# Forgetting attention with a SwiGLU block: more buffers for V's loads and a newly planned order of loads and units

## The chip, the cores and the metric

The kernel runs on one core of one Trainium2 chip. The metric is device time in microseconds (us) of one execution. Five engines work side by side, each through its own list of instructions in order: PE (TensorE, matmuls), DVE (VectorE), ACT (ScalarE), POOL (GpSimd) and SP (SyncE, which here only starts transfers). Semaphores join them.

## The reference, cut to what matters

There are 8 batches of 8 heads, a sequence of 576 and a head size of 64. The FFN has 4608 tokens (8 times 576), a model width of 512 (the 8 heads side by side) and an inner width of 1536.

```python
scores = (q @ k.T) / sqrt(D)
cum    = cumsum(log(clip(f, 1e-4, 1)), axis=-1)
scores = where(causal, -1e9, scores + cum[:, None] - cum[None, :])
attn   = exp(scores - max(scores)); attn = attn / (sum(attn) + 1e-9)
x      = (attn @ v), heads side by side: (4608, 512)
g      = x @ w_gate
out    = (g * sigmoid(g) * (x @ w_val)) @ w_out
```

## The kernel before, in words

**Units.** A pair `p` (0 to 31) is two heads of one batch; batch `b` has pairs 4b to 4b+3. Its 576 rows are cut into blocks of 64, both heads stacked on 128 partitions. A unit of attention is a pair and a half `g`: `g` = 0 are blocks 0 to 3, `g` = 1 are blocks 4 to 8. For a pair the kernel loads K, Q (`kf`, `qf`, line 409) and the cumulated gates spread over partitions (`cb`, line 418), casts K and Q to bf16 (`kb`, `qb`, lines 434 to 438), transposes them on PE (line 452) and copies them to `kt` and `qz` (lines 464, 466). Then, by unit:

- PE forms the scores in banks `sp` (line 498) and adds the mask (line 502).
- DVE adds the gates and takes the row minimum of the negated scores (`t`, line 526).
- ACT takes the exponential and the row sum (`e`, line 546).
- DVE or ACT adds the small constant to the sums (lines 560, 562), and DVE inverts (line 564).
- POOL, or ACT for early pairs, normalizes into `pk` (lines 580, 582).
- `pk` is transposed into `pT`: on PE for pairs 0 to 7 (line 612, copied by line 617), by a transposing transfer for later ones (line 595).
- PE multiplies with V (`vt`) into `tx` (line 638), and DVE or ACT copies the result into `xT` (line 662).

V comes in five pieces of up to 128 rows for each batch (`vf`, line 678), which POOL casts into `vt` (line 682).

Pair 0's `cb` is the exception: it is not transferred but spread by a matmul on the chip (line 393, copied by line 397). All other `cb` are read back from DRAM, where line 378 puts the cumulated gates.

**FFN.** The tokens are cut into tiles of 256, 256, seven times 512, 256, 128 and 128. For each tile PE computes gate and value products (`wg`, `wv`, line 720), ACT a tanh (line 726), DVE two products (lines 728, 731), PE the output product (line 748), and ACT or DVE copies it out (lines 755, 757), from where SP stores it (line 760). A tile can begin when all four pairs of its batch have written its rows. The weights arrive as bf16 through casting transfers that POOL starts (lines 695, 699): gate and value in four pieces each, cut at columns 0, 256, 512, 1024 and 1536 (named `wg0`, `wg2`, `wg4`, `wg8` by their first block of 128 columns; likewise `wv`), and the output weights in three.

**What sets the order.** All of this is first recorded as operations with a duration, a priority and candidate engines. `Plan.order` then plays the machine forward: it keeps a time for each engine and for the two transfer paths, gives each operation the earliest start that its inputs, its buffers and its engine allow, and so picks engine, buffer and place. The result is written out as a fixed order for each engine. So a constant that changes a planned time can move any operation after it. The constants that matter here:

- `COLD` (line 17): until this planned time, in ns, PE's durations count double.
- `STARTUP` (line 260): the order of the first loads. `p4` is K and Q of pair 4, `c4` its `cb`, `v03` piece 3 of V of batch 0, `wg4` a weight piece, `f9` the gates.
- `AHEAD` (line 250): a load of this list is planned no sooner than the one so many places ahead of it has landed. It is a rule of the plan, not a wait in the program.
- `NUDGE` (line 264): what is added to the priority of a unit. `a16.1` is attention of pair 16, half 1; `q12` loads and preparation of pair 12; `f8` gates of FFN tile 8; `o4` output of tile 4.
- `WAIT` (line 266): ns added to the planned start of a unit when the planner chooses between operations.

Buffers are real waits: a load into `vf` waits until the cast has read what the buffer held. `cm` (lines 299 and 475 to 483) holds gate sums with the mask added for pairs from `MFROM` on; `MFROM` is 32.

Of the kernel before, what the change touches and what calls it, by code (L numbers as in the profile page):

```python
# [8 lines left out]
F32 = mybir.dt.float32  # L9
# [4 lines left out]

BIG = 1.0e9
HUGE = 3.0e38
COLD = 25000
SLOW = 1.03


# [12 lines left out]
class Plan:  # L33
# [29 lines left out]
    def order(self):  # L63
# [72 lines left out]
        while ready:  # L136
# [18 lines left out]
            s -= o.bias.get(e, 0)  # L155
            if e == "PE" and s < COLD:
                dur *= 2
# [42 lines left out]
def kernel(  # L200
# [12 lines left out]
    B, H, S, D = q.shape  # L213
# [3 lines left out]
    P = 128  # L217
    QB = 64
    NB = S // QB
# [27 lines left out]
    NDIRECT = 0  # L247
    NSEL = 1
    MOST = (("p", 1), ("o", 2), ("f", 3))
    AHEAD = 7  # L250
    BEHIND = 6
    BOTH = 8
    LATER = {"DVE": 100}
# [3 lines left out]
    SOON = 8  # L257
    BACK = 4
    CBACK = 5
    STARTUP = "p0 f9 p1 c1 p3 p2 c2 v00 c3 wv0 wg2 wg0 wv2 v04 wv4 v01 v03 c4 wg4 v02 p4 wg8 wv8 v10 f0 p5 p6 c5 v14 c6 wo0 p7 wo4 v12 v13 v11 c7 wo8"  # L260
    HEAD = "10 00 20 30 11 01 31 21"


    NUDGE = "a10.0:1 a13.0:2 a15.0:-1 a15.1:-0.5 a16.1:-2 a20.0:-1 a21.0:1 a23.1:-1 a26.1:0.5 a27.1:-1.5 a28.0:1 a29.0:1 a31.1:10 f3:-4 f4:-7 f5:1 f6:2 f7:4.5 f8:4 f9:8 o6:-2.5 o8:2 q11:-2 q15:4 q22:5.5 q24:2.5"

    WAIT = ""
    ORDER = [(int(u[0]), int(u[1])) for u in HEAD.split()]
    ORDER += [(p, g) for p in range(len(ORDER) // 2, NPAIR) for g in (1, 0)]
    at = {u: n for n, u in enumerate(ORDER)}
# [8 lines left out]
    def bufs(name, shape, dtype, n, space=None):  # L278
        pl.pool(name, [(space or sb).tile(shape, dtype, name=f"{name}{x}") for x in range(n)])
# [16 lines left out]
    bufs("qz", [P, NB, 2, QB], BF16, 4)  # L296
    bufs("cb", [P, S], F32, 5)
    bufs("t", [P, S], F32, 4)
    bufs("cm", [P, NB, QB], F32, 2)
    for i in range(0, NB, 2):  # L300
        bufs(f"e{i}", [P, QB * (i + 2)], F32, 2)
    bufs("eo", [P, 512], F32, 4)
# [4 lines left out]
    for n in ("pk", "pT"):  # L307
        both[n] = [sb.tile([P, sum(NSL), P], BF16, name=f"{n}{x}") for x in range(2)]
        pl.pool(n + "1", [x[:, 0:NSL[1], :] for x in both[n]])
        pl.pool(n + "0", [x[:, NSL[1]:, :] for x in both[n]])  # L310
    bufs("vf", [P, H, D], F32, 2)
    bufs("vt", [P, 5, H, D], BF16, 2)
    bufs("th", [P, 512], F32, 3)
    bufs("hh", [P, 512], BF16, 18)
# [463 lines left out]
    line = []  # L778
    for x in STARTUP.split():
        n = int("".join(c for c in x if c.isdigit()))  # L780
# [14 lines left out]
    for n, o in enumerate(line):  # L795
        o.prio = -100 + n * .1
        if n >= AHEAD:
            o.after.append(line[n - AHEAD])
        if "POOL" in o.engs:
# [29 lines left out]

    nudge, leave = ({k: float(v) for k, v in (y.split(":") for y in x.split())} for x in (NUDGE, WAIT))  # L830
    for o in pl.ops:
# [38 lines left out]
```

## Time and profile before

| | us |
|---|---|
| median of 3 runs (lowest, highest) | 421.09 (419.6, 421.73) |
| the profiled execution's own time | 420.02 |
| its span, first to last instruction | 418.2 |

| engine | busy us | share of the span |
|---|---|---|
| PE (matmul) | 398.1 | 95% |
| DVE | 325.3 | 78% |
| ACT | 311.0 | 74% |
| POOL | 252.6 | 60% |

The profile is one execution. Busy time of PE includes the tail of each matmul, under which the next has begun, so it hides gaps shorter than that tail. "Idle before" a group of instructions is followed by what ended the wait. SP's own waits are those of its queue: while SP waits for one transfer's buffer or for an earlier transfer, all transfers behind it in its list wait too.

### The profile page before, as it was taken

How to read it: one execution, taken by the hardware profiler on the slowest of the kernel's cores; microseconds unless marked ns; L12 is line 12 of the kernel's file. 1: busy time of each engine (PE TensorE's matmuls, PEld its weight loads, DVE VectorE, ACT ScalarE, POOL GpSimd, SP SyncE). 2: the span in 40 equal slices, each digit the busy share in tenths (PEclk: the TensorE clock that was granted, in tenths of full speed). 3: DMA queues.
4: the chain of work that ended last, by engine and by line, in shares of the span. 5: the costliest groups of instructions: out<-in, count | busy, mean ns of one | idle time of the engine just before them, and what ended most of it. 6: DMA issues, size and time to landing. Idle time of an engine off the chain costs nothing.

```text
span 418.2 us, 9999 instructions
## 1 busy us (share of the span) xinstructions
PE 398.1 (95%) x3304; PEld 231.8 (55%) x3304; DVE 325.3 (78%) x1044; ACT 311.0 (74%) x875; POOL 252.6 (60%) x460
## 2 busy tenths in 40 slices
PE   1679999999999999999999999999999999999996
PEld 1446887665555555555555555555454444447875
DVE  4589999989998979889998979898866474553532
ACT  4689999999999978888987979899886332223321
POOL 7399977999788983886795787759784000000000
PEclk9999999999999999999999999999999999999999
DMA  7999999997999999999999999979976401001111
GB/s 176 203 166 235 220 214 206 224 236 183 204 229 212 232 197 237 204 237 199 225 216 226 228 235 210 234 189 208 221 155 146 88 2 51 25 27 50 52 52 52
DMA packets 143029, 72.22 MB, mean 173 GB/s; under 512 B 117761, under 2 KB 129793, under 8 KB 142977
## 3 DMA queue, kind: packets, MB, share of 16 engines
q1 hardware_dynamic: 136804, 66.27, 73.8%
q0 software_dynamic: 5808, 4.72, 7.7%
q10 hardware_dynamic: 364, 0.59, 0.6%
q8 instruction: 26, 0.43, 0.4%
q14 instruction: 27, 0.21, 0.2%
HBM read 47.04 MB, written 9.58 MB: 135 GB/s over the span
## 4 chain that ended last, share of the span: by engine, by line
PE 77%; DMA 7%; ACT 6%; POOL 4%; DVE 3%; issue 2%; SPq 0%; POOLq 0%; DVEq 0%; ACTq 0%
PE gv L720 38%; PE gv L748 20%; PE sp L498 8%; PE tx L638 5%; DMA kf<-in_k_dram 3%; PE tx L452 3%; POOL pk L582 3%; PE gv L612 2%; DMA pT<-pk 2%; DVE t L526 2%; ACT eo L546 2%; ACT e L546 2%; PE sp L502 1%; DMA cb<-cum_f 1%; DMA cum_f<-t 1%
## 5 line engine op out<-in xcount | busy, mean ns | idle before, releaser
L526 DVE CUSTOM_DVE_ANT_0 t<-sp,cb 128x512 f32<-128x512 f32 (+7 forms) x288 | 130.9, 475 | 13.5 <-PE sp L502 5.0
L582 POOL TENSOR_SCALAR pk<-e,lr 128x128 bf16<-128x128 f32 (+3 forms) x190 | 100.1, 530 | 32.7 <-DVE lr L564 15.1
L720 PE MATMUL gv<-xT,wv 128*128 128x512 bf16 (+2 forms) x576 | 111.4, 326 | 0.0
L720 PE MATMUL gv<-xT,wg 128*128 128x512 bf16 (+2 forms) x576 | 111.3, 326 | 0.0
L728 DVE SCALAR_TENSOR_TENSOR th<-th,gv 128x512 f32<-128x512 f32 x108 | 73.9, 685 | 43.7 <-ACT th L726 43.2
L748 PE MATMUL gv<-wo,hh 128*128 128x512 bf16 (+1 forms) x444 | 107.5, 374 | 0.0
L726 ACT ACTIVATE th<-gv 128x512 f32<-128x512 f32 x108 | 64.0, 592 | 42.1 <-PE gv L720 40.3
L546 ACT ACTIVATE e<-t,tm 128x448 f32<-128x448 f32 (+4 forms) x160 | 88.5, 555 | 4.6 <-DVE tm L526 3.9
L731 DVE TENSOR_TENSOR hh<-th,gv 128x512 bf16<-128x512 f32 x108 | 73.4, 685 | 9.0 <-PE gv L720 5.5
L498 PE MATMUL sp<-kt,qz 128*128 128x448 bf16 (+6 forms) x320 | 72.8, 295 | 3.8 <-DVE tm L526 3.7
L582 POOL TENSOR_SCALAR pk<-eo,lr 128x256 bf16<-128x256 f32 (+3 forms) x128 | 67.7, 530 | 12.4 <-DVE lr L564 4.9
L546 ACT ACTIVATE eo<-t,tm 128x256 f32<-128x256 f32 (+3 forms) x128 | 71.2, 557 | 4.3 <-DVE tm L526 2.2
L720 PEld LDWEIGHTS <-wv 128*128 128x128 bf16 x576 | 49.3, 98 | 34.8
L720 PEld LDWEIGHTS <-wg 128*128 128x128 bf16 x576 | 49.2, 98 | 35.0
L748 PEld LDWEIGHTS <-hh 128*128 128x128 bf16 x444 | 39.7, 98 | 37.1
L502 PE MATMUL sp<-mask,ident 128*128 128x64 bf16 x288 | 48.2, 197 | 0.0
L755 ACT ACTIVATE ot<-gv 128x512 f32<-128x512 f32 (+1 forms) x33 | 19.1, 581 | 36.7 <-PE gv L748 34.7
L498 PEld LDWEIGHTS <-qz 128*128 128x128 bf16 x320 | 31.0, 101 | 19.8 <-DVE qz L466 1.3
L436 POOL TENSOR_SCALAR qb<-qf 72x1024 bf16<-72x1024 f32 x30 | 31.2, 1041 | 8.8 <-DMA qf<-in_q_dram 6.1
L502 PEld LDWEIGHTS <-ident 128*128 128x128 bf16 x288 | 27.2, 100 | 15.2 <-issue 3.9
L546 ACT ACTIVATION_READ_ACCUMULATOR e<-t,tm 128x1 f32 x160 | 30.7, 192 | 0.0
L638 PE MATMUL tx<-pT,vt 128*64 128x320 bf16 (+4 forms) x448 | 29.4, 266 | 0.7 <-DMA pT<-pk 0.3
(60 smaller groups left out, 379.7 us busy)
## 6 DMA issues: line engine op xcount, KB each, us to landing
out_dram<-ot SPq DMA_DIRECT2D x35, 256.0 KB
kf<-in_k_dram SPq DMA_DIRECT2D x31, 288.0 KB
qf<-in_q_dram SPq DMA_DIRECT2D x31, 288.0 KB
cb<-cum_f SPq DMA_DIRECT2D x62, 144.0 KB
vf<-in_v_dram SPq DMA_DIRECT2D x32, 256.0 KB
wo<-in_moe_w_out_dram POOLq DMA_DIRECT2D x3, 512.0 KB, 9.2
vf<-in_v_dram SPq DMA_DIRECT2D x8, 128.0 KB
wv<-in_moe_w_val_dram POOLq DMA_DIRECT2D x2, 512.0 KB, 8.3
```

The source lines that it names most:

```text
L436: eng[e].tensor_scalar(dst, src, -scale, 1.0, op0=ALU.mult, op1=ALU.mult)
L498: nc.tensor.matmul(sp[:, o:o + z - a], qz[:, i, :, :].rearrange("p h r -> p (h r)"), kt[:, a:z], start=True, stop=not last or p >= MFROM)
L502: nc.tensor.matmul(sp[:, o - QB:o], ident, mask, start=False, stop=True)
L526: nc.vector.tensor_tensor_reduce(out=pl.buf(tk)[:, a:z], in0=pl.buf(sk)[:, o:o + z - a], in1=pl.buf(("cm", p))[:, i, :] if own else pl.buf ...
L546: nc.scalar.activation(pl.buf(ek)[:, :L], pl.buf(tk)[:, :L], AF.Exp, bias=pl.buf(("tm", p, g))[:, 0, i:i + 1], scale=-1.0, accum_out=pl.bu ...
L582: eng[e].tensor_scalar(dst, src, r, 1.0, op0=ALU.mult, op1=ALU.mult)
L638: nc.tensor.matmul(xo[r, 0:QB * n], vt[:, c, 2 * hp + h, :], pT[:, a:a + n, 64 * h:64 * h + 64], start=(c == 0), stop=(c == nch - 1))
L720: nc.tensor.matmul(pl.buf(bk)[:, j * n:j * n + n], wt[:, ko, fc * P:fc * P + P], xT[:, ko, x0:x0 + n], start=ko == 0, stop=ko == KD - 1)
L726: pl.op({"ACT": 487}, lambda e, u=u: nc.scalar.activation(pl.buf(("th", t, u)), pl.buf(("wg", t, u)), AF.Tanh, scale=0.5), [("wg", t, u)], ...
L728: pl.op({"DVE": 605}, lambda e, u=u: nc.vector.scalar_tensor_tensor(pl.buf(("th", t, u)), pl.buf(("th", t, u)), 1.0, pl.buf(("wg", t, u)), ...
L731: pl.op({"DVE": 605}, lambda e, u=u: nc.vector.tensor_mul(pl.buf(("hh", t, u)), pl.buf(("th", t, u)), pl.buf(("wv", t, u))), [("u", t, u), ...
L748: nc.tensor.matmul(pl.buf(bk)[:, 0:z - a], hh[:, (fc % nf) * n + ms * P:(fc % nf) * n + ms * P + P], wo[:, fc, a:z], start=fc == 0, stop=f ...
```

## The change

V's loads get four buffers in place of two, the buffers for masked gate sums are taken out, and five planner constants get other values, from which the planner makes a new order for all engines.

```diff
-COLD = 25000
+COLD = 31000
-    AHEAD = 7
+    AHEAD = 8
-    STARTUP = "p0 f9 p1 c1 p3 p2 c2 v00 c3 wv0 wg2 wg0 wv2 v04 wv4 v01 v03 c4 wg4 v02 p4 wg8 wv8 v10 f0 p5 p6 c5 v14 c6 wo0 p7 wo4 v12 v13 v11 c7 wo8"
+    STARTUP = "p0 f9 p1 c1 p3 p2 c2 wg0 v00 wg2 wv0 c3 wv2 v04 v03 wg4 wv4 c4 v01 p4 v02 wg8 v14 p5 wv8 p6 v11 c6 c5 v10 v13 p7 wo0 f0 wo4 wo8 v12 c7"
-    NUDGE = "a10.0:1 a13.0:2 a15.0:-1 a15.1:-0.5 a16.1:-2 a20.0:-1 a21.0:1 a23.1:-1 a26.1:0.5 a27.1:-1.5 a28.0:1 a29.0:1 a31.1:10 f3:-4 f4:-7 f5:1 f6:2 f7:4.5 f8:4 f9:8 o6:-2.5 o8:2 q11:-2 q15:4 q22:5.5 q24:2.5"
+    NUDGE = "a1.0:2 a10.0:1 a13.0:2 a15.0:-1 a15.1:-0.5 a16.0:2 a16.1:-2 a17.0:1 a17.1:1 a18.1:2 a20.0:-1 a21.0:1 a21.1:0.5 a23.1:-1.5 a25.1:-2.5 a26.0:2 a26.1:-0.5 a27.1:-1.5 a28.0:2 a29.0:1 a30.0:1 a30.1:-1 a31.1:10 f3:-4 f4:-7 f5:1 f6:2 f7:4.5 f8:7.5 f9:14 o4:-9 o5:-2 o6:-2.5 o8:2 q11:-2 q12:-4 q15:4 q21:-2 q22:-0.5 q24:2.5 q26:-2"
-    WAIT = ""
+    WAIT = "v2:100"
-    bufs("cm", [P, NB, QB], F32, 2)
-    bufs("vf", [P, H, D], F32, 2)
+    bufs("vf", [P, H, D], F32, 4)
```

Both programs hold the same 2674 planned operations. In the first part of the new order (by engine, before and after):

| engine | before | after |
|---|---|---|
| PE, from place 6 | scores of pair 1; K, Q of 2; K of 3; scores of pair 0 | K of 2; scores of pair 0; Q of 2; scores of pair 1; K of 3 |
| PE, first gate product of tile 0 | behind 39 operations | behind 47 operations |
| DVE, behind the cast of pair 3's Q | `t` of pair 1 | `t` of pair 0 |
| POOL, behind the casts of pair 1 | `kb` 2, `wv0`, `qb` 2, `wg2`, `pk` of pair 1 | `wg2`, `kb` 2, `qb` 2, `wg0`, `pk` of pair 0 |
| SP, first V loads | `v00 v04 v01 c4 c4 v03 v02` | `v00 v04 c4 v03 v01 c4 v02` |
| SP, then | Q, K of 4 and 5, `v10`, K, Q of 6 | K, Q of 4 and 5, half of `c5`, `v14 v11`, half of `c5`, K, Q of 6 |

## The prediction

> **What bounds the kernel now.** I read the busy times by stretch first, since a mean over the run hides its stages. The columns are the stretch in us, its length, the busy us of PE, PEld, DVE, ACT and POOL, the granted clock, the DMA share and GB/s.
>
> ```profile
> 0.00:10.00 10.00, 1.52 (x8) 1.24 (x9) 5.17 (x11) 4.60 (x6) 7.47 (x33) 1.00 0.70 171
> 10.00:20.00 10.00, 6.89 (x69) 5.15 (x68) 5.29 (x14) 5.45 (x14) 3.56 (x5) 1.00 0.99 213
> 20.00:30.00 10.00, 7.01 (x48) 4.45 (x47) 8.76 (x48) 9.31 (x37) 8.44 (x18) 1.00 1.17 160
> 30.00:40.00 10.00, 9.16 (x96) 6.64 (x96) 9.74 (x35) 9.41 (x26) 9.95 (x19) 1.00 1.16 228
> 40.00:50.00 10.00, 9.66 (x124) 8.01 (x122) 9.46 (x27) 9.63 (x26) 9.96 (x16) 1.00 1.17 235
> 50.00:60.00 10.00, 10.00 (x134) 8.36 (x133) 9.94 (x34) 9.47 (x27) 7.36 (x11) 1.00 1.04 196
> 60.00:80.00 20.00, 19.36 (x214) 15.19 (x211) 19.17 (x65) 19.16 (x53) 16.89 (x30) 1.00 1.07 218
> 80.00:320.00 240.00, 239.52 (x1964) 128.08 (x1963) 210.82 (x751) 213.89 (x640) 186.84 (x331) 1.00 1.03 214
> ```
>
> PE idles 20.1 us of 418.2: 8.5 + 3.1 + 3.0 + 0.8 + 0.3 + 0 + 0.6 = 16.4 us before 80 us, 0.5 us from 80 to 320, and 3.2 us after its last matmul. So only the opening has anything to give. From 20 to 60 us VectorE, ScalarE and GpSimd are all near full there: VectorE idles 1.24 + 0.26 + 0.54 + 0.06 = 2.1 us. Next come PE's waits: us in total, times, longest.
>
> ```profile
> PE tx L452 <- POOL kb L438: 8.5, 1, 8.5
> PE sp L498 <- DVE tm L526: 3.7, 9, 1.1
> PE tx L452 <- POOL qb L436: 2.5, 2, 2.3
> ```
>
> The 8.5 us are the first load and cast; their order is unchanged, so they stay. The 3.7 us are score banks that VectorE has not read yet. Then the timeline of the opening: start, duration, instruction, idle time before it and its releaser.
>
> ```profile
> 12.46 0.93 POOL L695 DMA_DIRECT2D wv<-in_moe_w_val_dram  x1
> 15.64 9.65 SPq L678 DMA_DIRECT2D vf<-in_v_dram  x3
> 16.30 1.04 POOL L436 TENSOR_SCALAR qb<-qf 72x1024 bf16<-72x1024 f32 x1 [2.91 <-DMA qf<-in_q_dram]
> 17.63 0.42 DVE L526 CUSTOM_DVE_ANT_0 t<-sp,cb 128x256 f32<-128x256 f32 x1 [1.43 <-DMA cb<-cum_f]
> 21.42 0.47 POOL L582 TENSOR_SCALAR pk<-eo,lr 128x256 bf16<-128x256 f32 x1 [3.33 <-DVE tm L526]
> 26.30 0.83 PE L612 MATMUL gv<-ident,pk 128*128 128x128 bf16 x6
> 31.67 0.50 PE L612 MATMUL gv<-ident,pk 128*128 128x128 bf16 x6
> ```
>
> VectorE waits for a cb transfer, GpSimd for pair 2's queries and then for the first softmax, and SP's third V load is held until a buffer is cast. The last two rows are equal work: 0.83 us, later 0.50 us. By the spacing of all matmul starts PE runs at half rate until 29.9 us and at full rate after, although the clock column says 1.00. Last, SP's own waits for V:
>
> ```profile
> SPq L678 <- DMA vf<-in_v_dram: 9.2, 4, 6.3
> SPq L678 <- POOL vt L682: 8.4, 8, 2.5
> ```
>
> **The change part by part.** The profiled execution took 420.02 us, the runs' median is 421.09: I work in the profile's time and add 1.07.
>
> No work is added or taken. All planned operations are the same in number; some move between VectorE, ScalarE and GpSimd. The masked gate buffers are unused in both programs (MFROM is 32, pairs are 0 to 31): price 0. The last tiles' PE order is equal, so the 3.2 us tail stays.
>
> (1) Opening order. Today VectorE's first score instructions are pair 1's and wait 1.43 us for its cb. Afterwards they are pair 0's, whose cb is made on chip by 11.8 us and whose queries are written by 15.5, so they start right behind the cast at 16.2 and end by 17.3 (four took 1.06). Behind them VectorE now has both query copies of pair 2 (0.76 each), which need PE's transposes (17.39 to 18.05), which need GpSimd's cast of 16.30. Counted at 20.8 us, VectorE has done 1.06 + 1.52 + 0.17 + 0.8 = 3.55 us of work against 3.27: a gain of 0.3. But GpSimd now issues the weight piece wg2 ahead of pair 2's two casts, at about 10.1 (behind the cast that ends at 10.08), not 12.46. Its 512 KB at the 213 GB/s of that stretch are 2.4 us. If all of it goes ahead of the queries that land at 16.1, the cast, the transposes, both copies and everything behind them on VectorE are late by that: +2.1. If none, -0.3. The first packets of wv came 1.6 us after its issue's start and most of them 3 to 5 us after, so part of wg2 moves beside the queries: I take 0.7 of delay, +0.4 net.
>
> On this the Trainium skill, page "DMA: Bandwidth & Descriptors", section "Issuing engines are not separate DMA queues", speaks against the change: transfers started from several engines share the same 16 DMA engines and interleave, so an early issue from GpSimd takes from SP's. A DMA share of 0.99 between 10 and 20 us agrees; by an equal split term (1) would be near +0.9, not +0.4.
>
> (2) PE's order. The program's order puts the first gate matmul behind 47 groups (planned operations of one or more matmuls), not 39: some 2.15 us of attention matmuls, at full rate, move ahead of it. The first 91 groups on PE are the same set in both, ending with tile 1's first pair of gate products (59.1 us today), so what counts is when the engines that feed this set are done. VectorE's first 108 operations differ by 6.5 us only before (two kt copies 1.5, hh 0.7, one qz 0.8, two pT 1.4 and one 0.6, lr 0.5, x 0.5, t 0.65) against 6.9 us only after (kt 0.8, three qz 2.3, pT 2.0, four x of about 0.4 scaled from 0.48, lr). Ends 0 and +0.8, taken +0.4.
>
> (3) Idle time of VectorE from 20 to 60 us. New orders may remove all 2.1 us or add as much as half again, 1.0. GpSimd, the fullest engine from 30 to 50, gets its first normalization earlier (21.42 could be 20 to 21), and two early normalizations go to ScalarE. I take half the idle time, -1.0.
>
> (4) Four V buffers. V loads behind the third no longer wait for a cast: SP's 9.65 us stretch ends sooner, and pair 4's inputs, cast at 42.4 today, land some us earlier. Until 50 us GpSimd is full, so earlier landings hide there. From 50 to 70 it waits 3.8 us for V in all, and PE loses 0.64 between 60 and 80. Ends -0.64 and 0, taken -0.5. The cover is the order: attention output of pair 4 now comes 12 us of PE work earlier and needs all five V pieces of batch 1, the last of which lands near 68 us today. If it lands no sooner, PE waits there instead, and the gain is gone.
>
> (5) Places of later units. At most 0.5 us can be won from 80 to 320. New waits like the 0.46 us that PE lost at 69 us for a query cast are the price: four of them, +2. The program leaves more PE work between scores and output for most pairs from 16 on (for 20: 27.7 us for 23.8), so I take 0. Weight pieces change places; today wg4 lands at 40.2 for a use at 42.6, and gates now start later: 0.
>
> Sum: +0.4 + 0.4 - 1.0 - 0.5 + 0 = -0.7, so 419.3, and 420.4 on the median's scale. About 0.5% (2.1 us) is what this kernel's measurement can tell from no change.
>
> **The rivals.** (A) The gaps go. The three full engines idle less, the queries are not late, V waits vanish: all terms at their low ends, -0.3 + 0 - 2.1 - 0.64 - 0.5 = -3.5, so 417.6. For it: every gap quoted above is a wait for a transfer or an order. Against it: three engines are above 94% at once, and one order must fill all.
>
> (B) Slower: PE changes to full rate later. Today dense gate matmuls start at 34.8, the change of rate comes at 29.9. With sparser PE work around 30 us, the rate could rise only when gates start. In 29.9 to 34.83 PE has 3.7 us of full-rate work today, 5.8 with the units moved ahead; at half rate that costs up to 5.8, about half of it hidden behind VectorE, so +3 on the forecast: 423.4. It decides from a change of rate later than about 33 us. Against it: PE's busy time in 20 to 30 is 7.0 us and the same score groups fill it afterwards. The Trainium skill, page "TensorE: Matmul & The Clock Gate", Part 1, gives this mechanism: the clock starts halved and is released by about 3.4 us of sustained activity in a free-running window. By that rule one missed window would be worth up to 3.4 us of full-rate work, an estimate; the two 612 rows agree with the two rates.
>
> (C) Nothing moves: transfers are held by the queue and not by the buffers (9.2 of SP's V waits are for earlier transfers, not casts), and feeding engines stay full: 421.0.
>
> **How the numbers follow.** The forecast with (C) beside it 0.40, within 0.5%; (A) 0.34, faster; slower 0.26, half of it (B), half late queries or new waits together. Low end: (A) less 1.0 for a change of rate some 3 us earlier (half of 3 us at 0.7 busy): 416.6. High end: (B) and the rest of (1), 1.2: 424.6.
>
> **What would show it.** Right: the first score instruction of VectorE near 16.2 to 16.5 without a cb wait; the query cast of pair 2 at 16.3 to 17.3; the first gate matmul at 37 to 40; tile 1's first gates near 58.5; SP's V waits for casts gone; PE idle after 80 us under 1 us. Wrong: the cast of pair 2 past 18, the rate change past 33 us, a PE wait of over 1 us for pair 4's output near 67 us, or PE waits of over 1 us for transposing transfers between 200 and 300 us.

## The result and the profile after

| | before | after |
|---|---|---|
| median of 11 runs each, same chip (lowest, highest), us | 420.9 (419.46, 428.02) | 423.57 (422.02, 424.93) |
| the profiled execution's own time, us | 420.02 | 423.45 |
| its span, us | 418.2 | 421.7 |

The ratio is 1.0065, with a 95% interval of 1.004 to 1.009: slower by 0.4 to 0.9%. The forecast was 420.4, no change that can be told from noise. One thing is needed to read the times below: of the 97 executions of before that the comparisons use, the 80 with a mean granted clock of 0.999 or more have a median of 420.06 us and the other 17 of 423.6, while those of after do not split so (five and six executions, medians 424.1 and 423.3); the profile of before is of the first kind.

The busy times by stretch of after, with the columns of the rows shown of before:

```profile
10.00:20.00 10.00, 6.20 (x59) 4.36 (x58) 5.43 (x14) 5.85 (x16) 3.20 (x4) 1.00 1.07 231
20.00:30.00 10.00, 7.24 (x55) 5.11 (x56) 8.19 (x43) 9.03 (x34) 6.60 (x14) 1.00 1.32 225
30.00:40.00 10.00, 8.05 (x66) 4.65 (x65) 8.99 (x37) 9.37 (x27) 9.77 (x18) 0.83 1.14 196
40.00:50.00 10.00, 10.00 (x128) 8.46 (x125) 8.87 (x25) 9.49 (x23) 9.89 (x17) 1.00 1.08 169
50.00:60.00 10.00, 9.91 (x132) 8.20 (x129) 9.76 (x31) 8.79 (x20) 6.44 (x9) 1.00 0.92 206
60.00:80.00 20.00, 18.09 (x204) 14.64 (x202) 18.00 (x61) 18.46 (x54) 17.26 (x30) 1.00 1.10 222
80.00:320.00 240.00, 240.00 (x1961) 128.94 (x1958) 208.40 (x731) 211.79 (x629) 180.73 (x318) 1.00 0.96 206
```

The long middle is full: PE idles 0 of 240 us, where it idled 0.48. All that is lost is lost before 80 us. VectorE (the third busy time) idles 1.81 + 1.01 + 1.13 + 0.24 = 4.2 us from 20 to 60, not 2.1. GpSimd (the fifth) does 6.60 us of work from 20 to 30, not 8.44. And the granted clock is 0.83 from 30 to 40.

The single instructions that the prediction named, from the timeline of after:

```profile
9.66 0.93 POOL L694 DMA_DIRECT2D wg<-in_moe_w_gate_dram  x1
16.45 0.42 DVE L525 CUSTOM_DVE_ANT_0 t<-sp,cb 128x256 f32<-128x256 f32 x1 [0.25 <-PE sp L501]
16.80 1.04 POOL L435 TENSOR_SCALAR qb<-qf 72x1024 bf16<-72x1024 f32 x1 [4.65 <-DMA qf<-in_q_dram]
35.61 0.62 POOL L681 CAST vt<-vf 128x512 bf16<-128x512 f32 x1
40.51 1.04 PE L719 MATMUL gv<-xT,wg 128*128 128x256 bf16 x8
77.45 1.02 PE L747 MATMUL gv<-wo,hh 128*128 128x512 bf16 x4 [1.91 <-DMA wo<-in_moe_w_out_dram]
```

VectorE starts its first scores at 16.45 without a `cb` wait, and the cast of pair 2's queries moves from 16.30 to 16.80. The row at 35.61 is the cast of piece 1 of V of batch 0, which had landed at 26.3: the new order puts it there. Every attention output of tile 0's tokens needs that piece. The first gate product starts at 40.51; before, the same row read:

```profile
34.83 1.03 PE L720 MATMUL gv<-xT,wg 128*128 128x256 bf16 x8
```

So the first gate product is 5.7 us later. The value half of tile 1's first pair of gate products, the last of the 91 groups that PE has in common up to there, starts at 62.18 for 59.10: 3.1 us later. The last output product starts at 417.80 for 414.39: 3.4 us later. So little is added behind 62 us, but this is a balance: PE has a new wait there of 1.9 us for the output weights, and the 1.1 us (0.64 + 0.48) that it idled from 60 to 320 in before are gone. PE's waits, and SP's wait for casts of V:

```profile
PE tx L451 <- POOL kb L437: 8.5, 1, 8.5
PE sp L497 <- DVE tm L525: 4.5, 10, 1.2
PE gv L747 <- DMA wo<-in_moe_w_out_dram: 1.9, 1, 1.9
PE tx L451 <- POOL qb L435: 1.4, 1, 1.4
SPq L677 <- POOL vt L681: 1.4, 1, 1.4
```

The score banks cost 0.8 us more. SP's waits for casts of V fell from 8.4 to 1.4 us; the next section shows that the buffers alone do not bring this.

### The profile page after: what moved, and what is told of

Read it like the earlier page. It is cut to its first block, busy times and chain, and to the rows that moved or that the text cites. A ratio compares the mean times of both kernels' runs of the same rounds, so it can differ in the third digit from the quotient of the medians.

```text
span 421.7 us, 9996 instructions
## 1 busy us (share of the span) xinstructions
PE 399.4 (95%) x3304; PEld 232.4 (55%) x3304; DVE 324.9 (77%) x1041; ACT 314.5 (75%) x880; POOL 251.4 (60%) x458
## 4 chain that ended last, share of the span: by engine, by line
PE 86%; DMA 7%; DVE 2%; ACT 2%; POOL 1%; issue 1%; SPq 0%; POOLq 0%; DVEq 0%
PE gv L719 42%; PE gv L747 22%; PE sp L497 9%; PE tx L637 6%; DMA wo<-in_moe_w_out_dram 4%; PE tx L451 3%; PE gv L611 3%; PE sp L501 2%; DMA qf<-in_q_dram 2%; DVE t L525 1%; DMA kf<-in_k_dram 1%; ACT e L545 0%; ACT eo L545 0%; DVE qz L465 0%; POOL kb L437 0%
## 5 line engine op out<-in xcount | busy, mean ns | idle before, releaser
L581 POOL TENSOR_SCALAR pk<-e,lr 128x512 bf16<-128x512 f32 (+3 forms) x189 | 99.5, 530 | 50.7 <-DVE lr L563 20.0
L747 PE MATMUL gv<-wo,hh 128*128 128x512 bf16 (+1 forms) x444 | 104.8, 374 | 1.9 <-DMA wo<-in_moe_w_out_dram 1.9
L581 POOL TENSOR_SCALAR pk<-eo,lr 128x384 bf16<-128x384 f32 (+2 forms) x127 | 67.5, 532 | 23.4 <-DVE lr L563 14.0
L497 PE MATMUL sp<-kt,qz 128*128 128x448 bf16 (+6 forms) x320 | 74.1, 297 | 6.3 <-DVE tm L525 4.5
```

What stands on the lines that cost most here:

```text
L497: nc.tensor.matmul(sp[:, o:o + z - a], qz[:, i, :, :].rearrange("p h r -> p (h r)"), kt[:, a:z], start=True, stop=not last or p >= MFROM)
L581: eng[e].tensor_scalar(dst, src, r, 1.0, op0=ALU.mult, op1=ALU.mult)
L747: nc.tensor.matmul(pl.buf(bk)[:, 0:z - a], hh[:, (fc % nf) * n + ms * P:(fc % nf) * n + ms * P + P], wo[:, fc, a:z], start=fc == 0, stop=f ...
```

## The experiments

Times are medians. Every ratio is to executions of before beside it on the same chip; their medians lay between 419.24 and 421.47. In the tables "first gate" is PE's first gate product and "tile 1" the value half of tile 1's first pair, both from that kernel's profile, which is one execution.

### The buffers alone

Before's order on every engine, with V's loads in four buffers in turn and `cm` out:

```diff
-    bufs("cm", [P, NB, QB], F32, 2)
+    more = [sb.tile([P, H, D], F32, name=f"vf{x}") for x in (2, 3)]
+    line_up = pl.order(); pl.pools["vf"] += more
+    for n, o in enumerate(o for o in line_up if o.eng == "SP" and o.writes[0][0] == "vf"):
+        pl.where[o.writes[0]] = n % 4
```

> The kernel before with its own order on every engine, but V's loads in four buffers in turn (the masked gate buffers are gone). If the buffers cost something by themselves (their earlier transfers crowd the weights and the queries in the opening), it is 1 to 3 us slower than before. If the loss lies in the order alone, it is within 0.7 us of before, and SP's waits of V loads for casts (8.4 us) are gone.

Measured: 420.17, ratio 0.9972 [0.9949, 0.9996]. The buffers are no loss, so all of the loss is in the new order. A gain is not shown either: all 12 executions here had a granted clock of 0.999 or more, and before's executions of that kind beside them have a median of 420.07. The second half of the expectation missed:

```profile
SPq L678 <- POOL vt L682: 7.4, 2, 4.7
```

SP's loads of V still wait 7.4 us for casts, for 8.4 in before. It is the new order that brings 1.4.

### Four suspects one by one, in after

PE's rate: 20 matmuls of 512 columns in PE's waits between 16.5 and 35.5 us, with results that nobody reads.

```diff
+    fill = {8: 3, 11: 1, 15: 1, 18: 3, 20: 2, 24: 1, 26: 1, ..., 34: 1}
+                for _ in range(fill.get(seen, 0)):
+                    nc.tensor.matmul(spare, ident, some[:, 0:512], start=True, stop=True)
```

> The changed kernel with 20 matmuls of 512 columns added on PE, put into its waits between 16.5 and 35.5 us; their product is not used. They hold PE's activity up. Theory 'rate': full rate comes earlier and does not fall back, PE's groups between 25 and 38 us take half as long, and the kernel gains 1.5 to 3 us. Theory 'feeding': the rate holds, but the first gate matmul moves by less than 0.8 us and the time by less than 0.7.

The weight piece `wg2` behind pair 2's casts on GpSimd:

```diff
+    move(("wg", 2), "POOL", ("qb", 2), "POOL")
```

> The changed kernel, with its first weight transfer on GpSimd (wg2, issued at 9.66) moved behind both casts of pair 2. If it makes pair 2's queries late, they land 0.5 us sooner (16.6 now), the cast on GpSimd starts near 16.2, and the time falls by 0.3 to 1. If queries do not wait for it, the time stays within 0.4.

Two normalizations of pair 1 from ScalarE back to GpSimd:

```diff
+    for o in line_up:
+        if o.writes == [("pk", 1, 0)]:
+            o.eng = "POOL"
```

> The changed kernel with its order, but the two normalizations of pair 1 that it gives to ScalarE (25.55 and 26.59 us) go back to GpSimd, which was idle from 24.2 to 25.7. Theory 'feeding' (engines in the opening wait for each other because operations stand in the wrong place): the exponentials behind them start 0.5 to 1 us sooner, VectorE's wait of 0.9 at 26.7 goes, and the kernel gains 0.5 to 1.2 us against the changed one. Theory 'rate' (what is lost is PE's return to half rate from 35.0 to 38.4): no gain beyond 0.4 unless the dip goes.

The first and second piece of the output weights swapped on GpSimd:

```diff
+    a, z = (next(n for n, o in enumerate(line_up) if o.writes[0] == ("wo", x)) for x in (4, 0))
+    line_up[a], line_up[z] = line_up[z], line_up[a]
```

> The changed kernel, with the transfers of the first and second third of the output weights in each other's place on GpSimd, so that the third that PE needs first is started first. If PE's wait of 1.9 us at 75.4 stands in the path, the kernel gains 1 to 1.9 us. If PE was ahead there and the wait only takes the place of later ones, it gains under 0.5.

| kernel | time | ratio to before | first gate | tile 1 |
|---|---|---|---|---|
| after | 423.57 | 1.0065 [1.004, 1.009] | 40.51 | 62.18 |
| after_fill | 424.49 | 1.0077 [1.0044, 1.011] | 39.77 | 61.68 |
| after_wg | 424.03 | 1.0065 [1.0037, 1.0093] | 40.71 | 62.38 |
| after_pk | 425.04 | 1.0074 [1.0037, 1.0111] | 42.06 | 63.73 |
| after_wo | 423.18 | 1.0047 [1.0018, 1.0076] | 40.86 | 62.53 |

None brings the time back. The swap of `wo` is a weak test: PE no longer waits for the first piece, but 1.3 us for the second, which now lands at 78.34. In the profiled execution of after_wg PE does not wait for `wo` at all, and that execution, 421.71, is the fastest of its twelve; so the 1.9 us of after may count in some executions, but the median of after_wg is no better. The rate is the instructive one. In after PE falls back to half rate, which the clock column shows; with the fillers it does not:

```profile
35.00:40.00 5.00, 4.70 (x48) 3.13 (x47) 4.44 (x18) 4.66 (x12) 5.00 (x9) 0.66 1.26 200
```

```profile
30.00:40.00 10.00, 8.89 (x82) 4.72 (x82) 9.63 (x37) 9.83 (x29) 9.95 (x18) 1.00 1.15 201
```

The first fence is after from 35 to 40, the second after_fill from 30 to 40. By bookkeeping the 3.1 us at tile 1 are 1.3 us more idle time and 1.7 us for a stretch of 3.4 us at half rate (35.0 to 38.4). Yet the run without that stretch starts tile 1 only 0.5 us earlier, and its total is no better: what PE gains it then waits, for engines that are hardly earlier (VectorE does 17.9 us of work from 20 to 40 us, 17.2 in after and 18.8 in before_v4). The spare matmuls stand in PE's list and may hide a gain of some tenths of a us. This clears the rate in after's order; what half rate costs in before's order no run here tests.

### A block of pair 1 earlier

Pair 1's last block and its inverse stand behind blocks of pair 2 in after. Moved ahead of them:

```diff
+    move(("m", 1, 1), "DVE", ("qz", 3))
+    move(("e", 1, 1), "ACT", ("qz", 3))
+    move(("lr", 1, 0), "DVE", ("m", 2, 0))
+    move(("l2", 1, 0), "DVE", ("pT", 0, 0))
+    line_up = merge(line_up)
```

`merge` gives out the buffers anew. Its control is the next kernel, `line_up = merge(line_up)` alone.

> After with four operations of pair 1's first half earlier on their engines: its last block's gate sum and minimum and its inverse on VectorE ahead of the blocks of pair 2 they stood behind, its last exponential and the sums' constant on ScalarE likewise; buffers handed out anew. Theory (the late inverse of pair 1 holds back GpSimd's normalizations, and with them the buffer of the exponentials and the whole line): pair 1's inverse at 22 to 23.5 in place of 25.3, first gate product at 38 to 39, total 421.5 to 423, 0.7 to 2 us under after. Rival (the line of VectorE is full and only changes what waits): first gate product at 40 to 41, within 0.5 us of after.

> After with every engine's order untouched, only buffers handed out anew in the way the three others have them (the least recently used one that is free). All theories: within 0.6 us of after, 423 to 424.2, first gate product at 40 to 41. If it differs by more, the three others must be read against it and not against after.

Measured: 423.72, 1.0067 [1.004, 1.0094], first gate at 40.66; the control 423.86, 1.006 [1.0025, 1.0095]. The control shows that new buffers do not change the time, though its first gate product comes at 42.55, 2.0 us later than in after and outside the 40 to 41 expected. The move does not change the time either. It brought pair 1's inverse forward, though less than the 22 to 23.5 expected; first after, then pair1, from VectorE's timeline:

```profile
25.33 0.18 DVE L563 RECIPROCAL lr<-lr 128x4 f32<-128x4 f32 x1
24.50 0.17 DVE L563 RECIPROCAL lr<-lr 128x4 f32<-128x4 f32 x1
```

So 0.8 us there are worth nothing at the end.

### The opening against the later order

One order's opening, up to tile 1's first pair, joined to the other's rest:

```diff
+    opening = [(1, 'DVE'), (3, 'POOL'), ...]   # operation and engine, in the other kernel's order
+    line_up = merge([pl.ops[n] for n, _ in opening] + [o for o in line_up if o.n not in early])
```

> After's order and engines for the operations that before plans up to tile 1's first pair of gate products, then before's order for the rest; V in four buffers. Theory (opening): 422.5 to 425, tile 1's first pair at 61.5 to 63.5. Rival (later order): 419 to 421.5.

> Before's order and engines for the operations that after plans up to tile 1's first pair of gate products, then after's order for the rest; V in four buffers, buffers handed out anew, both halves of a transposing transfer in one buffer. Theory (the loss is made in the opening): 419 to 421.5, tile 1's first pair at 58.5 to 61. Rival (the later order costs it): 422.5 to 425 with the same opening.

| kernel | opening | rest | time | ratio to before | tile 1 | last output product |
|---|---|---|---|---|---|---|
| before_v4 | before | before | 420.17 | 0.9972 [0.9949, 0.9996] | 61.06 | 415.12 |
| joined_new_old | after | before | 423.57 | 1.0071 [1.0047, 1.0095] | 63.15 | 418.23 |
| joined_old_new | before | after | 431.7 | 1.0251 [1.0217, 1.0285] | 60.16 | 426.61 |

The first two differ in the opening, and in buffers given out anew, which the control above clears. All of the loss is there: +3.4 us. The two ran on different chips; against before's executions at 0.999 or more beside them (420.07 and 420.14) they are at +0.1 and +3.4. At tile 1 the difference is 2.1 us, at the last output product 3.1: part of what the opening loses shows only behind tile 1. Its place by stretch, before_v4 first, joined_new_old second:

```profile
20.00:40.00 20.00, 15.78 (x149) 10.93 (x147) 18.79 (x80) 18.97 (x67) 17.09 (x33) 1.00 1.26 223
40.00:60.00 20.00, 18.76 (x247) 15.46 (x245) 18.57 (x55) 18.44 (x45) 17.68 (x27) 1.00 1.11 196
```

```profile
20.00:40.00 20.00, 16.09 (x108) 9.74 (x108) 17.14 (x77) 17.96 (x59) 16.27 (x32) 1.00 1.24 211
40.00:60.00 20.00, 19.91 (x262) 16.57 (x259) 18.28 (x50) 18.16 (x40) 17.55 (x27) 1.00 0.88 168
```

VectorE got 1.65 + 0.29 = 1.9 us less done with the new opening, ScalarE 1.3 us less. PE is busy for longer, but the profile has 26 matmuls fewer there: by the trace's clock records PE gets full rate at 40.2 us here and at 28.7 in before_v4. Equal transposes of joined_new_old show it, 14 in 1.70 us and then 8 in 0.62:

```profile
38.03 1.70 PE L612 MATMUL gv<-ident,pk 128*128 128x128 bf16 x14
40.34 0.62 PE L612 MATMUL gv<-ident,pk 128*128 128x128 bf16 x8
```

By after_fill the rate is not what costs the time: it is full there from 19.2 us on, with no gain. That leaves the engines that feed PE, which are late.

The third row of the table is no answer. Behind the seam GpSimd waits for a V piece in a place that suits neither order, and PE waits for GpSimd; without these 10 us it would be near 422, an estimate:

```profile
71.42 0.61 POOL L681 CAST vt<-vf 128x512 bf16<-128x512 f32 x1 [9.96 <-DMA vf<-in_v_dram]
72.76 0.29 PE L611 MATMUL gv<-ident,pk 128*128 128x128 bf16 x1 [9.76 <-POOL pk L581]
```

Four earlier joined kernels (old_open_new_rest 432.17, new_open_old_rest 428.65, splice_old_new 459.33, splice_new_old 487.67) and a first form of the pair 1 edit (after_pair1, 425.4) tell nothing: they gave some operations buffers of the wrong plan, so that part of the attention was computed from other data and much waited. In the splices the two halves of one transposing transfer got different buffers.

### The places of the first halves' last steps

In after the cast of V's piece 1, the transposes and copies of pairs 2 and 3, the `xT` copies and with them tile 0's gates stand behind second halves' scores. First these were taken earlier, then, in before with four buffers, later:

```diff
+    for o in line_up:
+        if first(o):          # the steps named above, and tile 0's wg, wv, th, u, hh
+            o.start += -4500  # before_late: +4500
+    line_up = merge(sorted(line_up, key=lambda o: (o.start, o.n)))
```

> After, with the last steps of the pairs' first halves and tile 0's chain 4.5 us earlier in the plan: the cast of V's piece 1 of batch 0, the transposes of pk and copies to pT of pairs 2 and 3, the attention outputs and x copies of pairs 0 to 3, and tile 0's wg, wv, th, u, hh; each engine's list is sorted anew by planned start, and buffers handed out as in after_merge. First gate product on PE behind 39 operations as in before, not 47. Theory (these steps, planned for a late V piece, stand behind second halves' scores, and PE has no gate products to fill its waits with): first gate product at 35 to 37.5, tile 1's first pair of gate products at 59 to 60.7, total 420 to 422. Rival (VectorE's list up to there is what counts, its sum and gaps; gates earlier only shift PE's waits): tile 1's first at 61.5 to 63, total 423 to 424.5.

> The opposite in before with four buffers for V (before_v4): the same steps 4.5 us later in the plan, so that the first gate product stands behind 45 operations on PE, not 39. Theory (places): first gate product at 39.5 to 42, total 422.5 to 425, 2.5 to 5 us over before_v4. Rival (VectorE's list): 419.5 to 421, as before_v4.

> As after_early, but the transposes of pair 2's pk stay where after has them (in after_early they stood ahead of their normalizations and held PE and with it VectorE for 3.3 us), and of tile 0's chain only units 0 to 3 are earlier. Against after, PE's order differs from place 28 to 66 only, VectorE's from 49 to 88, everything behind is the same. First gate product behind 39 operations, not 47. Theory (places of the first halves' last steps and the gates): first gate product at 35.5 to 37.5, tile 1's first pair at 59.3 to 61, total 420.5 to 422.5. Rival (VectorE's list decides, what PE does meanwhile only shifts its waits): tile 1's first pair at 61.7 to 62.7, total 423 to 424.5. If wv4 lands as late as in after (45.5), PE may wait up to 2 us for it near 44, which would hide part of a gain.

| kernel | time | ratio to before | first gate | tile 1 |
|---|---|---|---|---|
| after_early | 428.99 | 1.0195 [1.0163, 1.0226] | 38.80 | 68.29 |
| after_early2 | 427.68 | 1.0184 [1.0133, 1.0235] | 35.77 | 64.08 |
| before_late | 425.84 | 1.0124 [1.0087, 1.0161] | 38.85 | 62.73 |

after_early had a fault of its own: pair 2's transposes stood ahead of their normalizations, PE was held, and VectorE with it:

```profile
29.55 0.69 DVE L525 CUSTOM_DVE_ANT_0 t<-sp,cb 128x512 f32<-128x512 f32 x1 [3.27 <-PE sp L497]
```

after_early2 is without it. Its first gate product starts at 35.77, 4.7 us sooner than in after and as the theory said, and yet the kernel is 4 us slower. Two of PE's waits stand in its timeline in place of the gain:

```profile
46.59 1.05 PE L719 MATMUL gv<-xT,wv 128*128 128x256 bf16 x8 [1.27 <-DMA wv<-in_moe_w_val_dram]
81.34 1.87 PE L747 MATMUL gv<-wo,hh 128*128 128x512 bf16 x4 [3.90 <-DMA wo<-in_moe_w_out_dram]
```

The first wait is a gate product that now comes before its weights. By the landings in the traces, `wv4` is complete at 46.6 us here and at 45.5 in after, but at 35.2 in before: GpSimd issues it at 34.81 in after, not 28.38. The second is the output product, in its old place: the first piece of the output weights, issued at 64.14, is complete at 81.3 (77.4 in after, 63.2 in before), and behind it VectorE waited 5.0 us for scores. So the late gates of after stand in front of weights that also land late. Without the first wait tile 1 would start near 62.8 (64.08 less 1.27, an estimate), still no sooner than in after, so the theory that these places cost the time finds no support here. Whether late weights are what the order loses is looked at next.

before_late agrees only in part: late gates cost 5.7 us over before_v4, more than the 2.5 to 5 expected, in an order whose other places were not made for them.

### The order of the loads undone

```diff
-    STARTUP = "p0 f9 p1 c1 p3 p2 c2 wg0 v00 wg2 wv0 c3 wv2 v04 v03 ...
+    STARTUP = "p0 f9 p1 c1 p3 p2 c2 v00 c3 wv0 wg2 wg0 wv2 v04 wv4 ...
```

> After with one constant undone: STARTUP, the planned order of the first loads, as in before; COLD, AHEAD, NUDGE, WAIT and the four buffers as in after. The planner then casts V's piece 1 as the second V piece on GpSimd (place 46, not 51) and puts the first gate product behind 38 operations on PE, with pair 0's scores first as in after. Theory (the new order of loads makes the planner expect that piece late, and the places that follow cost the time): first gate product at 34.5 to 37, total 419 to 421.5. Rival (pair 0 first, or the other constants): 422.5 to 425.

Measured: 423.7, 1.01 [1.0065, 1.0134]. The first gate product is at 34.90, as early as in before, and the time is that of after. One of its waits, from PE's timeline:

```profile
44.53 1.05 PE L719 MATMUL gv<-xT,wg 128*128 128x256 bf16 x8 [2.27 <-DMA wg<-in_moe_w_gate_dram]
```

`wg4` lands at 44.5 here, 40.2 in before. Early gates wait for weights once more. But weights that land late do not by themselves make the loss. In before_v4, `wg4` lands at 44.6 and `wv4` at 41.4 (44.5 and 41.3 here), the first gate product starts at 35.82, PE waits less for `wg4`, and the kernel takes 420.17:

```profile
PE gv L720 <- DMA wg<-in_moe_w_gate_dram: 0.9, 1, 0.9
```

Nor does the late `wo`: in joined_new_old its first two pieces land at 65.6 and 69.1, PE never waits for them, and the whole loss is there.

### What is settled

Shown: the loss is in the order of the opening; it is not the four buffers, nor the later order, nor in after's order the rate, nor the place of `wg2`, of the two normalizations or of pair 1's last block alone. Shown too: starting the gates about as early as before, in two ways, does not bring it back. PE then waits for weight pieces, but before_v4 is fast with such weights and joined_new_old slow without a wait for `wo`, so these waits are not the loss. Open is the cause within the opening: VectorE and ScalarE get less done there, and no run shows which place in their lists does it.

## Why the prediction was wrong

Step by step, by its own terms:

- **(1) Opening order, +0.4.** The parts it saw came: scores at 16.45 without a `cb` wait, queries landed 0.5 us later (16.60 for 16.10) where 0.7 was taken. The mechanism is not shown: in after_wg `wg2` is issued at 18.07, not 9.66, and pair 2's queries landed at 16.91, no earlier. Over the other kernels they landed from 16.4 to 17.9 with `wg2` ahead and from 15.7 to 17.8 with it behind. By the Trainium skill ("DMA: Bandwidth & Descriptors", "Issuing engines are not separate DMA queues"), the transfers of several engines run on the same 16 DMA engines and interleave. The delay that the prediction took from this, 0.9 by an equal split, cannot be seen here. Its price was also too high: the profile lists `wg2` with the 256 KB that it writes, so by that count it is 1.2 us at 213 GB/s, not 2.4.
- **(2) PE's order and VectorE's sum, +0.4.** It counted the eight groups put ahead of the gates at PE's own 2.15 us and let the 91 groups pass as an equal set whose end VectorE's sum decides. The first gate product came 5.7 us later (40.51, past the 37 to 40 named), the end of the set 3.1 us later (62.18 for 59.10). That the place of the gates makes this is not shown: after_early2 and old_loads have early gates and stay slow.
- **(3) VectorE's idle time, -1.0.** This is the step that failed, in sign. "New orders may remove all 2.1 us or add as much as half again" was a range without a mechanism, and half of the good end was taken. The idle time from 20 to 60 us doubled, from 2.1 to 4.2: +2.1 for -1.0, a miss of 3.1 us where the total missed by 3.2 (423.57 for 420.4), though that the two agree is no proof. Taken together, (2) and (3) forecast -0.6 for what joined_new_old against before_v4 measures as +3.4. Which place in the opening makes VectorE idle stays open.
- **(4) Four V buffers, -0.5.** Not shown. In before_v4 SP's waits for casts went from 8.4 to 7.4 us only, and its 420.17 equals before's 420.07 at the same clock. The feared wait for pair 4's output near 67 us did not come. Of the 3.8 us that GpSimd waits for V in before, the base of this term, only 1.2 lie between 50 and 70.
- **(5) Later places, 0.** Right for the order behind the opening: PE idles 0 from 80 to 320, and joined_new_old, with before's rest, takes what after takes. Wrong for "weight pieces change places ... 0": `wv4` landed 10 us and the first piece of `wo` 14 us later, and PE waited 1.9 us for `wo`.

Rival (A) did not happen: the gaps grew. Rival (B) had the total (423.4 for 423.57), but by luck, for its mechanism is not what cost the time. The rate did move, from 29.9 to 31.6, with a second stretch of half rate to 38.4; in joined_new_old and after_pk, with nearly the same opening, full rate came at 40.2 and 40.6. But its price falls with after_fill: full rate from 19.2 us on, 0.5 us at tile 1, nothing in the total. The rule of the Trainium skill ("TensorE: Matmul & The Clock Gate", Part 1) fits how the clock moved, in windows of 3.4 us (31.6, 35.0, 38.4). Such a window at half rate can lose 1.7 us of full-rate work, half of the 3.4 that the prediction estimated. Rival (C) was the forecast's neighbour and fell with it.

## What to carry to other kernels

Where three engines are nearly full, the idle time that a new order makes is the main term, and half of the good end is no forecast of it. Work put earlier again can meet inputs that the new order brings late, and then be slower still (after_early2). Before such a wait is called the cause, look for a fast kernel that has it too: before_v4 had the late weights. To find where an order loses, join one order's opening to the other's rest with all else equal, and read the engine that has got less done. A mark on the way is not the total: after_merge starts tile 1 at 64.22, 2.0 us behind after, and takes the same time.

## What the runs showed of the hardware

- PE fell back to half rate after it had been at full rate for one window (31.6 to 35.0): the streamed columns of that window's matmuls make about 0.38 of it, an estimate from the trace (512 columns take 0.22 us). The same count gives 0.30 to 0.38 for the window behind which six other kernels fell back, and 0.42 (after_fill, from 19.2) and 0.47 (before_v4, from 28.7) for the emptiest early windows behind which the rate stayed. In before the emptiest had 0.70.
- The clock column reads 1.00 before the first change of rate, while PE runs at half rate: in joined_new_old until 40.2 us.
- A full rate 12 us earlier, bought with 20 spare matmuls, was worth nothing in a stretch that other engines feed.
- The first output weights took 15.2 us from issue to landing in after (62.24 to 77.41), right behind another 512 KB (issued at 61.07), and 9.3 in before (53.98 to 63.23), where they went first.
